# A planned attention-and-mixer kernel: a new order with two transfer lanes, V's parts and the output weights issued in pieces

## The chip, the cores and the metric

One core of a Trainium2 chip runs the kernel. The metric is the device time of an execution in microseconds; of several runs the median counts. Profiles come from one execution each, taken by the hardware profiler; its span is shorter than its time by what lies around the program.

## The reference

Four batches, 8 heads, 768 steps, head width 48. For each head a state of 48 x 48 decays by `w` at each step and takes in an outer product of `k` and `v`; the output reads the state with `r`, and the present step with the bonus `u`:

```
cur = u * k_t (outer) v_t
y_t = r_t @ (state + cur)
state = w_t * state + k_t (outer) v_t
```

The heads of `y` are laid side by side as `x` (4 x 768 x 384), and a token mixer follows: `wq = x @ w_q`, `wk = x @ w_k` (width 64), weights `wq @ wk.T / 8`, `mixed = weights @ x`, and `out = relu(mixed) @ w_out`. All inputs and the output are float32.

## The kernel before

The sequence is cut into 12 units of 256 steps (3 to a batch), each with two chunks of 128 steps. A unit loads 384 KB each of w, k, r and v (`wg`, `kg`, `rg`, `vg`; a partition holds two neighbouring steps of all heads). Then, per unit n:

- ACT takes the logarithm of w (`ln.n`, tile `lw`), PE sums it over time (`cw.n`), ACT makes two exponentials of the sums (`ep.n`, `en.n`).
- k, r and v are cast to bf16 (`k16.n`, `r16.n`, `v16.n`, mostly on POOL); PE turns k and r (`kT.n`, `rT.n`) and brings v into step order (`vp.n`, copied out as `VB.n`).
- DVE or POOL form the decayed factors: `ks`, `qT`, `RT`, `KT`. PE multiplies them (`A.n.c`), DVE masks the result (`AM.n.c`); `kb`, `kd`, `sn` and `SB` carry the state; `dps`, `dd` and `Vd` are the bonus term; `yi` (state) and `ya` (inside the chunk) are added to `Vd` as `X.n`.
- `X` is turned (`xt`, `XT`) and projected (`qk`, `QK` or `wqc`, `wkc`). After the third unit of a batch, `T` and `TS` (keys times x) follow, and for each unit of the batch `mx`, `rl` (relu, tile `MX`), `fp` (times `w_out`), `os` (copy out of PSUM) and the store `st`. A mixer unit `mx.m` uses the same numbers 0 to 11.

Unit 0 and unit 11 do some steps by chunk. Every wide matmul group has several ways, chosen by a letter: whole ("E") or as two halves of 64 columns ("e", "f").

All this is recorded as steps of a `Plan`. Each step names the engines that could do it with a cost in ns, the steps that it waits for, and the buffers that it reads and fills. Two tables hold the result of a search: `ALT`, a letter for the engine or way of each step that has a choice, and `RANK`, a place for each step. `Plan.order` sorts each engine's queue by rank, replays the queues with the costs, hands out PSUM banks, and so writes the program's order. Engines run their queues strictly in order; at run time only semaphores count, the costs do not.

All loads and nearly all stores are issued by SP, in one queue (`S`). A load may be issued once the cast of the unit four before has released its buffer (rings of four). In the plan a transfer is three steps: the issue on SP, the wire (`Q`) and the landing (`L`, 1950 ns). The old plan has a second wire lane (`R`) that is moved on by a fixed amount at each block of 128 PE instructions, and holds SP when the third-last transfer hasn't moved yet.

For units 2 to 11 V is loaded in three DMAs by partitions, 0 to 63, 64 to 126 and 127, one behind another. The weights `w_q`, `w_k` and `w_out` are three DMAs of one step (`wts`); POOL casts them (`wcast`). Thirty matmuls on a tile of zeros (`z`) are steps of the plan that keep PE busy early on.

Of the kernel before, what the change touches and what calls it, by code (L numbers as in the profile page):

```python
# [33 lines left out]
class Plan:  # L34
# [8 lines left out]
    ASIDE, BLOCKED = 1200, 1000  # L43
# [45 lines left out]
    def dma(self, key, issue, dur, fn, after=(), buf=None, reads=(), behind=None, high=None):  # L89

        i = self.add(key, {"S": issue}, fn, after, buf, lag=0, behind=behind)
        m = self.add(key + ("wire",), {"Q": (dur, dur if high is None else high, None)}, None, [i], lag=0)
        l = self.add(key + ("land",), {"L": self.LAND}, None, [m], lag=0, reads=reads)
        return i, l

    def order(self):
# [5 lines left out]
        wires = {}  # L102
# [6 lines left out]
        owners, moved, done, mode = [None] * 8, [], [], 0  # L109
# [14 lines left out]
        def start(s):  # L124
# [7 lines left out]
            if s["eng"] == "S" and len(moved) >= 3:  # L132
                t = max(t, moved[-3])
# [30 lines left out]
        while True:  # L164
# [5 lines left out]
            s = queues[e][place[e]]  # L170
# [24 lines left out]
            if lock:  # L195
                took += max(0, free["P"] - t)
            run(s, t, took)
            if lock:
                free["P"] = max(free["P"], t + took)
            if s["i"] in wires:  # L200
                m = wires[s["i"]]
                free["Q"] = max(free["Q"], s["end"]) + m["dur"]
                free["R"] = max(free["R"], s["end"]) + m["mode"]
                m["start"], m["end"] = s["end"], max(free["Q"], free["R"])
                done.append(m)
                moved.append(m["end"])
# [44 lines left out]
]  # L251
ALT = ("DDEDPEAEAPPEEEDEAeeEEeADPAEDPPeAEAPEEEAeEEEEDAPPEEEDPAeAEAPEEEAeEEEDAAEAEAEAEAEAEAPPEEED"
       "PPeAEDPEEEAeEEEEAAAPEEEAPAeDEAPEEEDEeEEEDAPPEEEAPPeAEAPEEEAEEEEDADEAEAEAEAEAeAPPEEEDPPEA"
       "EDPEEEAeeEEEDAPPEEEDPAEAEAPEEEAeeEEEDAPPEEEDPPeAeDPEEEAEEEEADAEAEAEAeDEAeDPPEEEDPPeAEAPE"
       "EEDeEEEEAAPPEEEDPPEAEDPEEEAEEEEeADPPEEEDPeAeDDPEEEAEEEEDDDeADDAeAEAeEDAeAeDEEDAeAeAEEDAE"
# [6 lines left out]
def kernel(  # L262
# [99 lines left out]
    def load(b, i, tl, ap, cuts=(0, C)):  # L362
        for p, z in zip(cuts, cuts[1:]):
            nc.sync.dma_start(  # L364
                out=view(tl, 0, [[D2, H], [1, D2]], p0=p, pn=z - p),
                in_=ap[b, :, ds(i * U + 2 * p, 2 * (z - p))].rearrange("h (p j) d -> p h (j d)", j=2))
# [114 lines left out]
    def weights():  # L481
        bq = Buf("none")

        def f(e):
            nc.sync.dma_start(out=view(wq_f, 0, [[DH, NK], [1, DH]]),
                              in_=moe_w_q.rearrange("(n p) h -> p n h", p=128))
            nc.sync.dma_start(out=view(wk_f, 0, [[DH, NK], [1, DH]]),
                              in_=moe_w_k.rearrange("(n p) h -> p n h", p=128))
            nc.sync.dma_start(out=view(wo_f, 0, [[DM, NK], [1, DM]]),
                              in_=moe_w_out.rearrange("(n p) d -> p n d", p=128))  # L490
        l = plan.dma(("wts",), 1800, 2700, f)[1]
# [5 lines left out]
        wts["qk"] = wts["o"] = add(("wcast",), {"P": 2650}, cast, [l])  # L497
# [7 lines left out]
    def unit(n, batch):  # L505
# [9 lines left out]
        for name, ap in (("wg", w), ("kg", k), ("rg", r)) + (() if whole else (("vg", v),)):  # L515
            g[name] = ring(name)
            cuts = (0, 64, 127, C) if name == "vg" and n in SPARE else (0, C)
            g[name + "L"] = plan.dma((name, n), 570 * (len(cuts) - 1) if "S" in begun else 1055,
                                     1220 if len(cuts) == 2 else 1730,
                                     lambda e, ap=ap, x=g[name].tile, cuts=cuts: load(b, i, x, ap, cuts),  # L520
                                     buf=g[name], behind=begun.get("S") if n == 0 else None,
                                     high=1220 if len(cuts) == 2 else 610)
# [162 lines left out]
        else:  # L685
# [4 lines left out]
                view(g["vg"].tile, 0, [[D2, H], [D, 2], [1, D]])), [g["vgL"]], v16, [g["vg"]])  # L690
# [244 lines left out]
        for ii in range(NU):  # L935
# [39 lines left out]
            for cs in halves:  # L975
# [8 lines left out]
                else:  # L984
                    plan.dma(("st", m, cs[0]), 400, 480 * len(cs), f_st, oss[cs], reads=[o])
# [70 lines left out]
```

## Time and profile before

| | |
|---|---|
| median of 3 runs | 106.12 us (105.59 to 106.23) |
| profiled execution | 106.6 us, span 104.8 us |
| busy share PE, PEld, DVE, ACT, POOL | 87, 63, 80, 76, 64% |
| share of the span in which the chain goes through PE, DMA, SP's queue | 38, 26, 9% |
| read and written in HBM | 19.66 and 4.72 MB |
| granted TensorE clock | 0.984 |

PE's busy time includes the `z` matmuls (39 of 128 x 512, 14.1 us). The chain is the work that ended last, followed back from the end: at each step to what released it. Times in the views are microseconds from the span's start, and "x3" counts instructions that a row merges. "Slices" are the 40 equal parts of the span on the page.

### The profile page before, as it was taken

Reading aid. Unit: us, or ns where it says so; the run is one execution under the profiler, and the core shown is the slowest. Engines: PE = TensorE matmul, PEld = TensorE weight load, DVE = VectorE, ACT = ScalarE, POOL = GpSimd, SP = SyncE. Lnnn points to the kernel's source line nnn. Section 1 sums busy time; section 2 is a strip of 40 time slices with the busy share of each in tenths; the row PEclk is TensorE's granted clock in tenths of the full one; section 3 lists DMA queues with packets and bytes.
Section 4 is the critical chain, followed back from the end, with each engine's and each line's share of the span. In section 5 each row is a group of like instructions: output and inputs, shape, how many; then the busy total and the mean of one; then the engine's idle time right before and its main releaser. Section 6 shows DMA issues by size and latency. Waiting matters only on the chain.

```text
span 104.8 us, 5072 instructions
## 1 busy us (share of the span) xinstructions
PE 91.6 (87%) x2201; PEld 65.7 (63%) x2201; DVE 84.3 (80%) x152; ACT 80.0 (76%) x117; POOL 66.9 (64%) x70
## 2 busy tenths in 40 slices
PE   6999998887699789999589689998999999999940
PEld 2264885485567558786375577865777778787510
DVE  5539999898699939999789699998999899857630
ACT  4359879989777298795996988999959898873830
POOL 4433695978998936988589779779995910400000
PEclk9999999999999957999999999999999999999999
DMA  1999997989999999889898999999989100029784
GB/s 33 317 323 325 325 318 183 282 228 244 264 315 267 235 298 248 215 199 280 226 228 199 248 304 307 222 317 301 304 283 326 43 0 6 6 111 367 274 287 172
DMA packets 53488, 24.71 MB, mean 236 GB/s; under 512 B 51162, under 2 KB 52314, under 8 KB 53466
## 3 DMA queue, kind: packets, MB, share of 16 engines
q1 hardware_dynamic: 53306, 24.19, 83.4%
q8 instruction: 17, 0.28, 1.1%
q10 hardware_dynamic: 160, 0.20, 0.5%
q14 instruction: 5, 0.04, 0.1%
HBM read 19.66 MB, written 4.72 MB: 233 GB/s over the span
## 4 chain that ended last, share of the span: by engine, by line
PE 38%; DMA 26%; SPq 9%; ACT 8%; POOL 6%; issue 5%; DVE 4%; POOLq 0%; ACTq 0%; DVEq 0%
PE PS L306 38%; DMA wg<-in_w_dram 13%; DMA vg<-in_v_dram 8%; SPq L364 8%; DMA kg<-in_k_dram 5%; ACT MX L466 3%; DVE AM L746 2%; POOL r L547 2%; POOL k L547 2%; POOL Vd L725 1%; ACT os L454 1%; ACT en L595 1%; SPq L977 1%; DVE VB L460 1%; ACT lw L536 1%
## 5 line engine op out<-in xcount | busy, mean ns | idle before, releaser
L746 DVE TENSOR_TENSOR AM<-PS,US 128x1024 bf16<-128x1024 f32 x24 | 29.0, 1220 | 2.8 <-PE PS L306 2.8
L725 POOL TENSOR_TENSOR Vd<-VB,dd 128x768 bf16<-128x768 bf16 (+1 forms) x13 | 17.6, 1353 | 8.3 <-DVE dd L460 6.1
L663 POOL TENSOR_TENSOR KT<-ks,en 128x1024 bf16<-128x1024 bf16 x10 | 21.3, 2129 | 0.8 <-ACT ep L589 0.7
L595 ACT ACTIVATE en<-PS,dn 128x1024 bf16<-128x1024 f32 (+1 forms) x14 | 13.9, 992 | 2.9 <-PE PS L306 2.4
L306 PE MATMUL PS<-Z 128*128 128x512 bf16 (+1 forms) x43 | 14.8, 432 | 1.1 <-DVE Z L380 1.0
L536 ACT ACTIVATE lw<-wg 128x768 bf16<-128x768 f32 x12 | 10.1, 842 | 6.3 <-DMA wg<-in_w_dram 6.2
L589 ACT ACTIVATE ep<-PS,up 128x1024 bf16<-128x1024 f32 (+1 forms) x14 | 13.9, 1011 | 1.0 <-PE PS L306 0.8
L306 PE MATMUL PS<-wo,MX 128*128 128x384 bf16 (+1 forms) x93 | 13.8, 327 | 0.3 <-ACT MX L466 0.3
L306 PEld LDWEIGHTS <-KT 48*128 48x128 bf16 x352 | 9.1, 95 | 6.9 <-issue 4.0
L547 POOL CAST k<-kg 128x768 bf16<-128x768 f32 x10 | 8.3, 825 | 6.0 <-DMA kg<-in_k_dram 4.7
L851 DVE TENSOR_TENSOR X<-PS,Vd 128x768 bf16<-128x768 f32 (+1 forms) x13 | 11.5, 892 | 0.7 <-PE PS L306 0.4
L306 PE MATMUL PS<-RT,KT 48*128 48x128 bf16 x192 | 9.9, 220 | 1.4 <-ACT QK L454 0.9
L466 ACT ACTIVATE MX<-PS 128x768 bf16<-128x768 f32 (+1 forms) x14 | 9.4, 700 | 1.9 <-PE PS L306 1.9
L687 POOL CAST v<-vg 128x768 bf16<-128x768 f32 x9 | 7.4, 827 | 4.3 <-DMA vg<-in_v_dram 4.1
L547 POOL CAST r<-rg 128x768 bf16<-128x768 f32 x10 | 8.3, 827 | 2.3 <-DMA rg<-in_r_dram 2.3
L650 DVE TENSOR_TENSOR RT<-PS,ep 128x1024 bf16<-128x1024 bf16 (+1 forms) x14 | 8.4, 607 | 1.6 <-PE PS L306 1.4
L454 ACT CAST VB<-PS 128x768 bf16<-128x768 f32 x11 | 8.9, 807 | 1.0 <-issue 0.6
L454 ACT COPY os<-PS 128x768 f32<-128x768 f32 (+1 forms) x10 | 7.0, 702 | 3.3 <-PE PS L306 2.1
L306 PEld LDWEIGHTS <-MX 128*128 128x128 bf16 (+1 forms) x93 | 7.1, 103 | 3.5 <-ACT MX L466 0.4
L306 PE MATMUL PS<-CM,lw 64*128 64x128 bf16 x192 | 8.2, 231 | 1.2 <-ACT lw L536 1.0
L641 DVE TENSOR_TENSOR qT<-PS,ks 128x1024 bf16<-128x1024 bf16 x12 | 8.2, 683 | 0.4 <-PE PS L306 0.3
L809 DVE TENSOR_TENSOR SB<-PS,ep 128x192 bf16<-128x192 f32 x20 | 7.0, 350 | 1.8 <-PE PS L306 1.7
(88 smaller groups left out, 184.9 us busy)
## 6 DMA issues: line engine op xcount, KB each, us to landing
wg<-in_w_dram SPq DMA_DIRECT2D x12, 384.0 KB
kg<-in_k_dram SPq DMA_DIRECT2D x12, 384.0 KB
rg<-in_r_dram SPq DMA_DIRECT2D x12, 384.0 KB
out_dram<-os SPq DMA_DIRECT2D x9, 384.0 KB
vg<-in_v_dram SPq DMA_DIRECT2D x10, 192.0 KB
vg<-in_v_dram SPq DMA_DIRECT2D x10, 189.0 KB
out_dram<-os SPq DMA_DIRECT2D x5, 192.0 KB
vg<-in_v_dram SPq DMA_DIRECT2D x2, 384.0 KB
```

Source lines behind the costliest of these rows:

```text
L306: return nc.tensor.matmul(o, l, rr, start=start, stop=stop, skip_group_check=True, is_transpose=trans)
L454: nc.scalar.copy(o, i)
L466: nc.scalar.activation(o, i, ACT.Relu)
L536: nc.scalar.activation(view(lw.tile, 0, [[64, H], [512, 2], [1, D]]), view(g["wg"].tile, 0, [[D2, H], [D, 2], [1, D]]), ACT.Ln, bias=0.0, ...
L547: op(view(o.tile, 0, [[64, H], [512, 2], [1, D]]), view(g[src].tile, 0, [[D2, H], [D, 2], [1, D]]))
L589: nc.scalar.activation(view(ep.tile, cs[0] * NP * EW + RS, [[EW, n4], [1 - RS, 2], [1, R]]), view(at(cw), cs[0] * 512, [[C, n4], [R, 2], [ ...
L595: nc.scalar.activation(en.tile[:, ds(cs[0] * 512, w_)], at(cw)[:, ds(cs[0] * 512, w_)], ACT.Exp, bias=dn, scale=-1.0)
L650: nc.vector.tensor_tensor(view(RT.tile, cs[0] * 512, [[512, len(cs)], [R, H], [1, R]]), view(at(kr, BF16), cs[0] * apart + second, [[apart ...
L663: x.tensor_tensor(KT.tile[:, w], ks.tile[:, w], en.tile[:, w], ALU.mult)
L725: (nc.vector if e == "D" else nc.gpsimd).tensor_tensor(Vd.tile[:, cols], VB.tile[:, cols], view(dd.tile, cs[0] * H, [[1, len(cs) * H], [0, ...
L746: AMs[c] = add(("AM", n, c), {"D": 1221}, lambda e, c=c, A=A: nc.vector.tensor_tensor(view(AM[c].tile, 0, [[C, 8], [1, C]]), view(at(A), 0 ...
L851: lambda e, c0=c0, nc_=nc_: nc.vector.tensor_tensor(view(X.tile, (2 * i + c0) * DM, [[D2, NP * nc_], [D, 2], [1, D]]), view(at(y), c0 * NP ...
```

## The change

The computation, the tiles and the rings stay. What changes:

- The plan's model of transfers: two lanes, each with a depth (`DEEP`); an issue on SP lasts until both lanes have room. A load takes 1220 ns on lane Q and 1500 on lane R, which stands for the slower engine; the fixed delay at each PE block goes.
- V's three parts are steps of their own, in the order 64 to 126 (`vl`), 127 (`vk`), 0 to 63 (`vg`), so that other transfers can stand between them. Only `vg` takes time on lane R.
- `w_out` is loaded in three DMAs, rows 0 to 62, 63 to 125, 126 to 127 of each of three blocks, as a step of its own (`wtso`) behind `w_q` and `w_k` (`wts`).
- `RANK` and `ALT` are new: the order of every engine and the choice of engine for many steps.

```
-    ASIDE, BLOCKED = 1200, 1000
+    DEEP = dict(Q=1850, R=2500)
...
-            if s["eng"] == "S" and len(moved) >= 3:
-                t = max(t, moved[-3])
...
-                    free["R"] = max(free["R"], cross + self.ASIDE) + self.BLOCKED
...
+            if s["i"] in wires:
+                m = wires[s["i"]]
+                x = t + took
+                full = [0]
+                for q, d in (("Q", m["dur"]), ("R", m["mode"])):
+                    if d:
+                        free[q] = max(free[q], x)
+                        full.append(free[q] + m["opts"]["Q"][5] * d // max(m["dur"], 1) - self.DEEP[q])
+                        free[q] += d
+                m["start"] = x
+                m["end"] = max([x] + [free[q] for q, d in (("Q", m["dur"]), ("R", m["mode"])) if d])
+                took = max(took, max(full) - t)
...
-            nc.sync.dma_start(out=view(wo_f, 0, [[DM, NK], [1, DM]]),
-                              in_=moe_w_out.rearrange("(n p) d -> p n d", p=128))
-        l = plan.dma(("wts",), 1800, 2700, f)[1]
+        def f_o(e):
+            for p, z in ((0, 63), (63, 126), (126, 128)):
+                nc.sync.dma_start(out=view(wo_f, 0, [[DM, NK], [1, DM]], p0=p, pn=z - p),
+                                  in_=moe_w_out.rearrange("(n p) d -> p n d", p=128)[ds(p, z - p)])
+        l = [plan.dma(("wts",), 1000, 700, f, deep=900, high=850)[1],
+             plan.dma(("wtso",), 1500, 3300, f_o, high=0, deep=800)[1]]
...
+            if name == "vg" and n in SPARE:
+                g["vl"] = [plan.dma(("vl", n), 500, 1065, lambda e, f=f: f(e, p0=64, p1=127),
+                                    buf=g[name], high=0)[1]]
+                g["vl"].append(plan.dma(("vk", n), 500, 20, lambda e, f=f: f(e, p0=127, p1=C),
+                                        buf=g[name], high=0)[1])
+                g["vgL"] = plan.dma((name, n), 500, 610, lambda e, f=f: f(e, p0=0, p1=64),
+                                    buf=g[name], high=750)
```

The order of SP's transfers that follows from the tables, by step (numbers are units; `v` in the old order is V in three parts from unit 2 on):

```
before: wg0 kg0 rg0 vg0 wg1 kg1 rg1 kg2 wg2 vg1 rg2 v2 wg3 wg4 kg3 v3 rg3 wts kg4 rg4 wg5 v4
  kg5 rg5 wg6 kg6 rg6 v5 v6 wg7 rg7 kg7 v7 wg8 v8 rg8 kg8 wg9 rg9 kg9 wg10 v9 wg11 kg10
  rg10 rg11 kg11 v10 st2 st1 v11 st0 st4 st6 st5 st3 st7 st8 st9.1 st9.0 st10.0 st11.1 st10.1
after:  wg0 kg0 rg0 vg0 wg1 kg1 vg1 rg1 kg2 wg2 vl2 rg2 vk2 vg2 rg3 wg3 wts kg3 wtso wg4 vl3
  vk3 vg3 kg4 rg4 vl4 wg5 vg4 vk4 kg5 rg5 wg6 kg6 rg6 vl5 vl6 vk6 vg5 vk5 vg6 wg7 rg7 kg7
  vl7 vk7 vg7 kg8 rg8 vl8 vk8 wg8 vg8 wg9 rg9 kg9 vl9 kg10 vl10 vk9 vk10 wg10 vl11 vg9
  vg10 rg10 rg11 wg11 kg11 vk11 vg11 st3 st0 st5 st4 st2 st6 st1 st7 st8 st9.0 st9.1 st10.0
  st11.1 st10.1
```

The last pieces of the other queues that the prediction speaks of (POOL, ACT, from the third-last unit's end on):

```
POOL before: v16.10 Vd.9 r16.11 v16.11 k16.11 Vd.10 Vd.11.1
POOL after:  v16.10 Vd.9 v16.11 r16.11 Vd.10 k16.11 Vd.11.0 Vd.11.1
ACT before:  ln.11 dd.9 os.3 os.4 kd.10 XT.8 VB.10 QK.7 en.11 ...
ACT after:   ln.11 os.3 XT.7 kd.10 os.4 QK.7 VB.10 ep.11 QK.8 ...
DVE after:   X.9 X.10 KT.11.0 ks.11 SB.10.1 RT.11.0 RT.11.1 KT.11.1 qT.11 kd.11 AM.11.0 SB.11.0 AM.11.1 X.11.0 X.11.1
```

KT of units 1, 3 and 7 stands on DVE and not on POOL; XT of units 1, 4, 5 and 7 on ACT and not on DVE (8 the other way); fp of ten units instead of four goes in halves.

More of the change, by code (lines that the diff above doesn't have):

```diff
@@ L87, in add, with dma @@
         return s
-    def dma(self, key, issue, dur, fn, after=(), buf=None, reads=(), behind=None, high=None):
+    def dma(self, key, issue, dur, fn, after=(), buf=None, reads=(), behind=None, high=None,
+            deep=None):
         i = self.add(key, {"S": issue}, fn, after, buf, lag=0, behind=behind)
         m = self.add(key + ("wire",), {"Q": (dur, dur if high is None else high, None)}, None, [i], lag=0)
+        m["opts"]["Q"][5] = dur if deep is None else deep
         l = self.add(key + ("land",), {"L": self.LAND}, None, [m], lag=0, reads=reads)
@@ L108, in order @@
         rings = {k: [] for k in self.rings}
-        owners, moved, done, mode = [None] * 8, [], [], 0
+        owners, done, mode = [None] * 8, [], 0
         count, edge, ready = 0, self.FIRST, 0
@@ L196, in order @@
                 took += max(0, free["P"] - t)
+            if s["i"] in wires:
[10 more added lines that the diff above has]
+                took = max(took, max(full) - t)
+                for q, d in (("Q", m["dur"]), ("R", m["mode"])):
+                    if d:
+                        free[q] = max(free[q], t + took)
+                        m["end"] = max(m["end"], t + took)
             run(s, t, took)
@@ L200, in order @@
             if s["i"] in wires:
[L201 to L204, printed above, removed]
                 done.append(m)
-                moved.append(m["end"])
                 x = wires[m["i"]]
@@ L216 @@
 RANK = [
[34 rows of a table removed]
-]
[L252 to L255, printed above, removed]
[36 rows of a table added]
+]
+ALT = ("DAeDPeAEDDDEeeAEAeeeEEADPAEDDPEAEAPEEEAeeEEEAAAPEEEDPPeAEDPEEEAeEEEDAAEAEAEAEAEAEAPAEEED"
+       "DPeAEAPEEEAEeEEEAAPPEEEAPAEDEAPEEEDeeEEEAAPPEEEAPPEAEDPEEEAEEEEAAAeAEAEAeAEAeAPPEEEDPPeA"
+       "EDPEEEAEEEEEDAPPEEEDDPEAEDPEEEAeeEEEAAPPEEEAPPEAEAPEEEAEEEEDAAEAEAeDeDeAeAPPEEEDPPeDEDPE"
+       "EEDeEEEeAAPPEEEDPPeAEDPEeEAEEEEeAAPPEEEDPeAEAPPEEEDEEEEAAAfDADAeAeAeeADeDEDeeADeDEDeeDAE"
        "EEEEEEEEEEEEEEEEEEEEEEEEEEEEE")
@@ L360, with load @@
     dn = const([C, 1], F32, "dn")
[L362 to L366, printed above, removed]
+    def load(b, i, tl, ap, p, z):
+        nc.sync.dma_start(
+            out=view(tl, 0, [[D2, H], [1, D2]], p0=p, pn=z - p),
+            in_=ap[b, :, ds(i * U + 2 * p, 2 * (z - p))].rearrange("h (p j) d -> p h (j d)", j=2))
     def load_whole(b, q, tl):
@@ L496, in cast @@
             nc.gpsimd.tensor_copy(wo_sb, wo_f)
-        wts["qk"] = wts["o"] = add(("wcast",), {"P": 2650}, cast, [l])
+        wts["qk"] = wts["o"] = add(("wcast",), {"P": 2650}, cast, l)
         ut = bank()
@@ L516, in unit, with f @@
             g[name] = ring(name)
[L517 to L522, printed above, removed]
+            def f(e, ap=ap, x=g[name].tile, p0=0, p1=C):
+                load(b, i, x, ap, p0, p1)
+            t, issue, rest = 1220 if n < 2 else 1500, 500 if "S" in begun else 1055, None
+            if name == "vg" and n in SPARE:
[5 more added lines that the diff above has]
+                                    buf=g[name], high=750)
+            else:
+                g[name + "L"] = plan.dma((name, n), issue, 1220, f, buf=g[name], high=t,
+                                         behind=begun.get("S") if n == 0 else None)
             if n == 0:
@@ L689, in unit @@
                 view(v16.tile, 0, [[D, H], [DM, 2], [1, D]]),
[L690 removed]
+                view(g["vg"].tile, 0, [[D2, H], [D, 2], [1, D]])), [g["vgL"]] + g.get("vl", []), v16,
+                [g["vg"]])
             def f_vp(e):
@@ L984, in unit @@
                 else:
-                    plan.dma(("st", m, cs[0]), 400, 480 * len(cs), f_st, oss[cs], reads=[o])
+                    plan.dma(("st", m, cs[0]), 400, 480 * len(cs), f_st, oss[cs], reads=[o],
+                             deep=80 * len(cs), high=560 * len(cs))
     batch = None
```

70 rows, old and new, of the table RANK are left out of this document.

## The prediction

> **What bounds the kernel now.** I read the page first (busy shares, slices, queues), then the chain that ended last, then the time lines of SP, POOL, ACT and DVE around the places that the chain names, and the order in which both programs' instructions stand on each engine.
>
> ```profile
> span 104.8 us, 5072 instructions
> PE 91.6 (87%) x2201; PEld 65.7 (63%) x2201; DVE 84.3 (80%) x152; ACT 80.0 (76%) x117; POOL 66.9 (64%) x70
> ...
> GB/s 33 317 323 325 325 318 183 282 228 244 264 315 267 235 298 248 215 199 280 226 228 199 248 304 307 222 317 301 304 283 326 43 0 6 6 111 367 274 287 172
> ...
> q8 instruction: 17, 0.28, 1.1%
> ```
>
> No engine is full; the transfers lead. One slice is 104.8/40 = 2.62 us; counted from 0, slices 1 to 5 run at about 325 GB/s, slices 6 to 30 mostly do not: their shortfalls against 325 add up to 1603 GB/s, and 1603/325 x 2.62 = 12.9 us of holes before the last input has landed. The 17 packets of the instruction queue took 1.1% of 16 engines' span, 0.011 x 16 x 104.8 = 18.4 us, over 1 us each; the views don't part the sixteen engines, so that one or two carry them is an assumption here.
>
> ```profile
> 27.62 8.40 DMA wg<-in_w_dram
> ...
> 44.80 4.94 DMA wg<-in_w_dram
> ...
> 55.70 5.12 DMA kg<-in_k_dram
> ...
> 76.68 4.35 DMA vg<-in_v_dram
> ...
> 81.18 0.06 POOL v L687
> ...
> 81.95 0.84 POOL k L547
> ...
> 82.83 3.39 PE PS L306 x94
> ```
>
> The chain (start, us, what) goes through loads again and again and leaves them for good at 76.68 + 4.35 = 81.03, when the last part of unit 11's V lands. POOL then casts V and K, and PE takes K. After 81.03 there are 23.8 us of pure computation and stores.
>
> ```profile
> 5.37 1.15 SPq L364 DMA_DIRECT2D kg<-in_k_dram  x1
> 6.56 1.15 SPq L364 DMA_DIRECT2D rg<-in_r_dram  x1
> ...
> 17.54 2.54 SPq L364 DMA_DIRECT2D kg<-in_k_dram  x1
> ...
> 25.51 0.49 SPq L489 DMA_DIRECT2D wof<-in_moe_w_out_dram  x1
> ...
> 73.88 1.45 SPq L977 DMA_DIRECT2D out_dram<-os  x2
> 75.38 1.99 SPq L364 DMA_DIRECT2D vg<-in_v_dram  x3
> 77.41 24.22 SPq L977 DMA_DIRECT2D out_dram<-os  x12
> ```
>
> SP's own time line (start, us): in the steady stretch a 384 KB load is issued every 6.56 - 5.37 = 1.2 us, the pace of the wire (393 KB at 325 GB/s is 1.21 us). An issue of 2.54 us is SP held by a full queue; nothing behind it can be issued, though other DMA engines may be idle. That is how holes arise. Two stores stand ahead of the last V.
>
> **The change part by part.**
>
> *Stores leave the load stream.* The new SP order has all 14 of its stores behind the last load; before, two of 384 KB stood ahead of it. Two times 1.21 us off the wire: the last V lands 2.4 us earlier (lower bound the 1.45 us of SP). The stores that move to the end are covered by a wire that is nearly empty (slices 31 to 34: 43, 0, 6, 6).
>
> *Output weights in three.*
>
> ```profile
> wof<-in_moe_w_out_dram SPq DMA_DIRECT2D x1, 576.0 KB
> ```
>
> 590 KB at 325 GB/s is 1.8 us. The trace has no such pieces alone. If the 63-row pieces are slow, the nearest rows are the slices in which V's three-part loads stand thickest, at 199 GB/s: 590/199 = 3.0 us, or +1.2. If they bypass an engine that also fetches instructions, that engine gains up to its 1.8 us. Two more issues at 0.49 are +1.0 us of SP, hidden while the queue is full. I take 0, with ends -1.8 and +1.2.
>
> The Trainium skill (DMA: Bandwidth & Descriptors, "Why a DMA increments its semaphore by 16 and not by 1") says that such a copy uses the largest number of engines up to 16 that divides the slowest dimension on both sides, so 63 rows run on nine; an estimate by it is 1.8 x 126/128 x 16/9 = 3.2 us on those nine and nothing on the other seven, beside the 3.0 us from the 199 GB/s slice. The same page's "Rules for kernel authors" calls a split of a transfer over partitions useless and wants one of 128 partitions; by that rule this part is the +1.2. The low rate of the slices with V in parts speaks for it, the slow instruction queue against it.
>
> *Parts of V issued apart, new load order.* The 63-row part now goes first, often with another load before the 64-row part (vl.4, wg.5, vg.4; vl.9, kg.10, vl.10). SP should be held less by one lagging engine. What this is worth can only be bounded: nothing of the 12.9 us of holes, or all that the computation could follow:
>
> ```profile
> 10.00:90.00 80.00, 72.19 (x1926) 54.10 (x1926) 71.50 (x110) 67.25 (x97) 61.45 (x53) 0.98 0.90 238
> ```
>
> DVE (the third figure) is idle 80 - 71.5 = 8.5 us between 10 and 90, so that is the ceiling. Against that, the q and k weights now precede unit 3's K, the output weights its V, and wg.11 comes late: a loss of a load or so, up to 1.5 us, is possible. I take 1.5 us gained, nearer the low end, since every load still moves the same bytes.
>
> *Work moved between engines.*
>
> ```profile
> L663 POOL TENSOR_TENSOR KT<-ks,en 128x1024 bf16<-128x1024 bf16 x10 | 21.3, 2129 | 0.8 <-ACT ep L589 0.7
> ...
> L454 ACT COPY XT<-PS 128x768 bf16<-128x768 bf16 x5 | 4.0, 794 | 0.2 <-PE PS L306 0.2
> ...
> L650 DVE TENSOR_TENSOR RT<-PS,ep 128x1024 bf16<-128x1024 bf16 x10 | 6.8, 684 | 1.6 <-PE PS L306 1.4 <-issue 0.3
> ...
> L460 DVE COPY XT<-PS 128x768 bf16<-128x768 bf16 x6 | 3.3, 551 | 0.1
> ```
>
> KT of units 1, 3 and 7 goes from POOL (3 x 2.13 = 6.4 us less) to DVE. DVE on two SBUF operands isn't in the trace; between 0.68 (RT) and POOL's 2.13 I take 0.7, as DVE's other 1024-column products do: +2.1. Four whole XT go to ACT and one comes back: 3 x 0.55 = 1.65 off DVE, 3 x 0.79 = 2.4 on ACT. The small casts and relus (0.2 to 1.0 us each) about cancel on DVE. So DVE gains under 1 us, ACT some 3, POOL loses over 6; with 8.5 and 12.8 us idle between 10 and 90, DVE and ACT hide this (if ACT's cover is gone, up to 3 us).
>
> *The order at the end.*
>
> ```profile
> 79.22 0.82 POOL L547 CAST r<-rg 128x768 bf16<-128x768 f32 x1
> 81.18 0.83 POOL L687 CAST v<-vg 128x768 bf16<-128x768 f32 x1 [1.13 <-DMA vg<-in_v_dram]
> 81.95 0.83 POOL L547 CAST k<-kg 128x768 bf16<-128x768 f32 x1
> 82.74 1.48 POOL L725 TENSOR_TENSOR Vd<-VB,dd 128x768 bf16<-128x768 bf16 x1
> ...
> 75.13 0.83 ACT L536 ACTIVATE lw<-wg 128x768 bf16<-128x768 f32 x1
> ...
> 78.81 0.82 ACT L456 ACTIVATE kd<-PS 128x768 bf16<-128x768 bf16 x1
> 79.52 0.81 ACT L454 COPY XT<-PS 128x768 bf16<-128x768 bf16 x1
> 80.19 0.83 ACT L454 CAST VB<-PS 128x768 bf16<-128x768 f32 x1
> ...
> 89.07 0.80 ACT L454 COPY os<-PS 128x768 f32<-128x768 f32 x1 [0.25 <-PE PS L306]
> ...
> 86.35 0.96 DVE L851 TENSOR_TENSOR X<-PS,Vd 128x768 bf16<-128x768 f32 x1 [0.15 <-PE PS L306]
> 87.22 0.35 DVE L809 TENSOR_TENSOR SB<-PS,ep 128x192 bf16<-128x192 f32 x1
> ...
> 90.01 0.17 DVE L460 COPY dd<-PS 128x16 f32<-128x16 f32 x1
> 90.21 0.56 DVE L725 TENSOR_TENSOR Vd<-VB,dd 128x384 bf16<-128x384 bf16 x1
> 91.03 1.02 DVE L851 TENSOR_TENSOR X<-PS,Vd 128x384 bf16<-128x384 f32 x2 [0.26 <-PE PS L306]
> ...
> 90.78 1.14 PE L306 MATMUL PS<-wo,MX 128*128 128x384 bf16 x6
> ```
>
> POOL waited only 1.13 us for the last V, so an earlier landing alone is worth 1.13. Its new order is v, r, Vd.10, k of unit 11: k now stands behind Vd.10, which needs VB.10 from ACT. ACT's new order puts os.3, XT.7, kd.10, os.4, QK.7 and VB.10 behind ln.11, which waits for wg.11; and wg.11 is now the load third from last, with only kg.11 and V's last half behind it (1.2 + 0.6 = 1.8 us).
>
> The sum: the last V lands at 81.03 - 2.4 - 1.5 = 77.1, wg.11 at 75.3. From ln.11 to the end of VB.10 ACT has 4.9 us of work (ln 0.83, four copies at about 0.70 from one start to the next, as 78.81 to 79.52, a smaller one below that, VB 0.83), so VB.10 ends at 80.2 (81.02 before). Vd.10 holds POOL until 81.65, k starts there instead of 81.95: 0.3 earlier. Behind K's transposes DVE now has X.10 and the last dd and Vd out of its way: from PE's start on K at 82.83 to the end of X.11 at 92.05 it took 9.2 us; without X.10 (0.87 from start to start) and the dd, Vd and waits between 90.01 and 91.03 (some 0.9), plus a kd (0.3), 7.7 are left: -1.5. On PE one fp of 1.14 us (fp.6) leaves the stretch ahead of T.11 and another (fp.7) enters the one behind it: they nearly cancel, I take +0.2. Together -0.3 - 1.5 + 0.2 = -1.6 on the span of 104.8: 103.2.
>
> The profiled execution took 106.6 us beside its span of 104.8, and the runs' median is 106.12 (105.59 to 106.23), so the forecast is 106.12 - 1.6 = 104.5. About 1% is what a measurement of this kernel tells from no change.
>
> **The rivals.**
>
> *wg.11 comes too late (slower).* Mechanism: ACT stands at ln.11 with VB.10 behind it, POOL at Vd.10 with K behind it, PE at kT.11. By the sum above, each us that the load stream loses delays kT.11 by one; the change breaks even when the last V lands at about 78.7. If the new order gains nothing, and loses 1.2 by the weights and 1.0 by loads that come late, the last V lands at 81.03 - 2.4 + 2.2 = 80.8, wg.11 at 79.0, VB.10 ends at 83.9, K starts at 85.4: +3.4 - 1.3 = +2.1, 108.2. For it: in the old stream five more loads, two stores and a V stood behind wg.11, now hardly two; against it: the stores are gone.
>
> *Nothing comes through (same).* The split and the new order buy nothing: the last V lands at 78.6 for the stores alone, wg.11 at 76.8, VB.10 ends at 81.7, K starts at 83.1: +1.2 - 1.3 = -0.1, 106.0. For it: the same bytes go through the same engines, and the 2.4 us fall into a POOL that waited 1.13. Against it: the holes that SP's long issues show.
>
> *The holes close (much faster).* If half of DVE's 8.5 idle us between 10 and 90 go, the end comes 4 us earlier: 102.1. For it: chain pieces of 8.40, 4.94 and 5.12 us in loads. Against: seven stores of 384 KB and six of 192 KB then stand on SP from st.5 on, and os.5 was done at 89.07 + 0.80; at the 367 GB/s of slice 36 their 3.9 MB take 10.7 us, so the span can hardly end before 101.
>
> **How the numbers follow.** Forecast 104.5 (0.36), slower rival 108.2 (0.29), same at about 106 (0.20), holes close 102.1 (0.15). The range 102.0 to 108.2 takes in the unknown bounds of the order (-1.5 to +4 us around none); the likeliest case's own range is 103.4 to 105.2. Faster by over 1%: 0.36 + 0.15 = 0.51; within: 0.20; slower: 0.29.
>
> **What would show it.** Right: in the new profile no store before the last V, V of unit 11 landed by 77.5, wg.11 before 75.5, POOL's k of unit 11 started before 82, fewer slices under 250 GB/s. Wrong: ln.11 with a wait of more than 2 us for wg, the last V after 78.7, ACT or PE waits of several us around the weights at 22 to 30 us, or a tail behind kT.11 as long as before.

## The result, and the profile after

The new kernel takes 112.45 us (median of 4 runs, 110.96 to 113.24), the old one beside it 106.18: the ratio is 1.056 [1.042, 1.071], slower. The forecast was 104.5, with 108.2 as the end of the range.

The profiled execution took 113.24 us, 0.8 above the median, with a span of 111.4. Its first loads, of the same size as before, already ran slower (counted from 0, slice 3 at 253 GB/s, before 325), so the sizes are taken from the comparisons of medians below and only the places from this profile. A ratio leaves out runs that lie over 1.5% above the fastest of their kernel, so it can differ from that of the medians shown. The page's lines on span, engines, granted clock and transfers, and the shares of the chain by engine:

```profile
span 111.4 us, 5210 instructions
PE 93.9 (84%) x2272; PEld 67.9 (61%) x2272; DVE 84.4 (76%) x151; ACT 82.6 (74%) x121; POOL 60.4 (54%) x67
PEclk9999999999996569999999997699999999999999
GB/s 42 320 296 253 306 232 209 281 277 203 134 210 290 188 250 243 296 181 226 303 175 288 234 249 218 218 185 246 305 273 152 150 6 0 201 286 234 173 363 169
SPq 37%; DMA 22%; PE 21%; POOL 7%; issue 6%; ACT 3%; DVE 0%; POOLq 0%; ACTq 0%
```

The engines have nearly as much to do as before (PE and ACT 2.3 and 2.6 us more, DVE the same), and POOL 6.5 us less, about as counted. What grew is the part of the chain in which SP stands in an issue: 37% against 9% before. The new hole is at slice 10 (28 us): 134 GB/s.

The chain of waits (start, us, what):

```profile
25.38 4.87 SPq L375
...
72.11 3.69 DMA wg<-in_w_dram
...
76.62 6.32 DMA wg<-in_w_dram
...
82.96 0.34 ACT lw L558
...
95.11 12.60 PE PS L318 x298
```

Before, the chain left the loads with the last V. Now it leaves them with unit 11's gate weights, which land at 76.62 + 6.32 = 82.94, and goes on through ACT's logarithm and then through PE. POOL's cast of unit 11's K, which stood in it before, is no longer in it. SP's time line shows the two issues around the output weights, and the 14 stores behind the last load:

```profile
22.24 1.80 SPq L503 DMA_DIRECT2D wof<-in_moe_w_out_dram  x3
...
24.61 6.35 SPq L375 DMA_DIRECT2D vg<-in_v_dram  x3
...
79.69 1.99 SPq L375 DMA_DIRECT2D vg<-in_v_dram  x2
84.52 24.13 SPq L1000 DMA_DIRECT2D out_dram<-os  x14
```

ACT's time line, unit 5's logarithm and the end, and then POOL's end, the same instructions as in the prediction's fence:

```profile
41.16 0.84 ACT L558 ACTIVATE lw<-wg 128x768 bf16<-128x768 f32 x1 [0.98 <-DMA wg<-in_w_dram]
...
82.96 0.85 ACT L558 ACTIVATE lw<-wg 128x768 bf16<-128x768 f32 x1 [0.46 <-DMA wg<-in_w_dram]
...
87.63 0.80 ACT L465 CAST VB<-PS 128x768 bf16<-128x768 f32 x1
```

```profile
86.50 0.82 POOL L709 CAST v<-vg 128x768 bf16<-128x768 f32 x1
87.27 0.83 POOL L569 CAST r<-rg 128x768 bf16<-128x768 f32 x1
88.51 1.48 POOL L748 TENSOR_TENSOR Vd<-VB,dd 128x768 bf16<-128x768 bf16 x1 [0.41 <-ACT VB L465]
89.93 0.82 POOL L569 CAST k<-kg 128x768 bf16<-128x768 f32 x1
```

From K's start to the end of the span it is 111.4 - 89.93 = 21.5 us (before 104.8 - 81.95 = 22.9): the tail did get shorter. K starts 8.0 us later than before.

### The profile page after: what moved, and what is told of

It is laid out like the page before. It is cut to its first block, busy times and chain, and to the rows that moved or that the text cites. A ratio compares the mean times of both kernels' runs of the same rounds, so it can differ in the third digit from the quotient of the medians.

```text
span 111.4 us, 5210 instructions
## 1 busy us (share of the span) xinstructions
PE 93.9 (84%) x2272; PEld 67.9 (61%) x2272; DVE 84.4 (76%) x151; ACT 82.6 (74%) x121; POOL 60.4 (54%) x67
## 4 chain that ended last, share of the span: by engine, by line
SPq 37%; DMA 22%; PE 21%; POOL 7%; issue 6%; ACT 3%; DVE 0%; POOLq 0%; ACTq 0%
SPq L375 34%; PE PS L318 21%; DMA wg<-in_w_dram 9%; DMA kg<-in_k_dram 5%; DMA rg<-in_r_dram 4%; DMA vg<-in_v_dram 4%; POOL KT L685 2%; SPq L503 2%; POOL r L569 1%; SPq L496 1%; POOL Vd L748 1%; POOL k L569 1%; ACT lw L558 1%; POOL v L709 1%; ACT os L465 1%
## 5 line engine op out<-in xcount | busy, mean ns | idle before, releaser
L318 PE MATMUL PS<-Z 128*128 128x512 bf16 (+2 forms) x45 | 15.5, 431 | 1.1 <-DVE Z L391 1.0
L685 POOL TENSOR_TENSOR KT<-ks,en 128x1024 bf16<-128x1024 bf16 x7 | 14.9, 2130 | 2.6 <-ACT ks L465 1.6
L318 PE MATMUL PS<-wo,MX 128*64 128x384 bf16 (+1 forms) x114 | 13.7, 328 | 0.0
L709 POOL CAST v<-vg 128x768 bf16<-128x768 f32 x11 | 9.1, 826 | 8.2 <-DMA vg<-in_v_dram 7.5
L318 PE MATMUL PS<-CM,lw 64*128 64x128 bf16 (+1 forms) x208 | 7.9, 231 | 5.4 <-ACT lw L558 2.9
L318 PEld LDWEIGHTS <-KT 48*128 48x128 bf16 (+1 forms) x376 | 9.5, 98 | 3.9 <-issue 1.6
L318 PE MATMUL PS<-RT,KT 48*128 48x128 bf16 (+1 forms) x208 | 9.8, 224 | 0.6 <-POOL KT L685 0.5
L318 PEld LDWEIGHTS <-lw 64*128 64x128 bf16 (+1 forms) x208 | 6.2, 105 | 6.7 <-ACT lw L558 5.0
L318 PEld LDWEIGHTS <-MX 128*64 128x64 bf16 (+1 forms) x114 | 7.1, 106 | 3.3 <-issue 0.2
L477 ACT ACTIVATE MX<-PS 128x768 bf16<-128x768 f32 (+1 forms) x10 | 7.4, 750 | 1.9 <-PE PS L318 1.9
```

Of the source, the lines that this page charges most:

```text
L318: return nc.tensor.matmul(o, l, rr, start=start, stop=stop, skip_group_check=True, is_transpose=trans)
L685: x.tensor_tensor(KT.tile[:, w], ks.tile[:, w], en.tile[:, w], ALU.mult)
L709: v16s = add(("v16", n), {"P": 826, "A": 810}, lambda e: (nc.scalar.copy if e == "A" else nc.gpsimd.tensor_copy)(view(v16.tile, 0, [[D, H] ...
```

## The experiments

Each kernel is the one before or after with one part exchanged. "Loads" means the order on SP; the engines' order (PE, ACT, DVE, POOL, with the choice of engine) goes apart from it. Every ratio is to the kernel before, run beside it on the same chip. None leaves work out.

### 1 to 4: pieces, loads, engines

**1. After, output weights whole.**

```
-            for p, z in ((0, 63), (63, 126), (126, 128)):
+            for p, z in ((0, 128),):
```

> The changed kernel with w_out loaded in one DMA of 128 rows at the place of the three; all orders else kept. Weights theory (the two 63-row pieces hold the load stream for some 3 us between 24 and 30 us, and all that follows is late by it): 108 to 110 us, SP is not held for 4.9 us behind them, wg of unit 4 lands near 29 instead of 31.7. Order theory (the new order of engines and loads costs the time wherever the weights stand): 111.5 to 113, as the changed kernel.

110.51 us (109.48 to 111.05), ratio 1.040 [1.031, 1.050]. The kernel after stood at 1.056 [1.042, 1.071]. So the pieces look like a part of the loss and not the whole of it; but the two intervals overlap, and run 2 is the clearer measure.

**2. Before, output weights in pieces.** The same edit the other way round, in the kernel before.

> The kernel before with nothing changed but w_out in the three DMAs of the change. Weights theory: 108 to 109.5 us, K of unit 4 lands 2 to 3 us later than at 31.25. Order theory: 105.5 to 106.8, since the DMA engines have room there.

110.77 us (110.03 to 111.58), ratio 1.045 [1.036, 1.054]. This one edit, counted at nothing, costs 4.6 us, more than either theory had. POOL's time line, first of the kernel before, then of this one:

```profile
30.87 1.15 POOL L496 CAST wo<-wof 128x1152 bf16<-128x1152 f32 x1
32.49 0.83 POOL L547 CAST r<-rg 128x768 bf16<-128x768 f32 x1 [0.47 <-DMA rg<-in_r_dram]
```

```profile
32.89 1.15 POOL L497 CAST wo<-wof 128x1152 bf16<-128x1152 f32 x1 [1.40 <-DMA wof<-in_moe_w_out_dram]
37.24 0.83 POOL L548 CAST r<-rg 128x768 bf16<-128x768 f32 x1 [3.20 <-DMA rg<-in_r_dram]
```

The weights' cast is 2.0 us late, but the R behind them 4.75. The landing records of the trace (one for each part of a transfer, sixteen for a load of 128 rows) divide this in two. The whole stream is shifted: K of the same unit is 2.55 us late, and fifteen of R's sixteen parts 2.3 (34.64 against 32.37). R's last part comes only at 37.19, 2.55 behind the fifteen. Such a late part is not the pieces' own: in before, the last part of unit 5's gate weights landed 2.1 us behind the others (36.02 against 33.93). SP's time line, of before and of this kernel, shows why the loss spreads:

```profile
27.62 2.34 SPq L364 DMA_DIRECT2D wg<-in_w_dram  x1
30.06 2.71 SPq L364 DMA_DIRECT2D vg<-in_v_dram  x3
```

```profile
26.04 1.24 SPq L490 DMA_DIRECT2D wof<-in_moe_w_out_dram  x3
...
28.49 3.89 SPq L364 DMA_DIRECT2D wg<-in_w_dram  x1
32.47 4.91 SPq L364 DMA_DIRECT2D vg<-in_v_dram  x3
```

The issues of the pieces are short; the two loads behind K and R hold SP for 3.89 and 4.91 us instead of 2.34 and 2.71. The view of the transfers from 24 to 34 us, of the kernel before and of this one:

```profile
DMA packets 6403, 2.77 MB, mean 277 GB/s; under 512 B 6017, under 2 KB 6401, under 8 KB 6401
```

```profile
GB/s 223 197 237 246 264 287 289 208 146 65 60 241 172 90 48 107 135 197 233 227 203 234 253 301 233 221 181 183 198 174 157 171 206 298 321 297 237 224 284 293
DMA packets 4583, 2.08 MB, mean 208 GB/s; under 512 B 4197, under 2 KB 4581, under 8 KB 4581
```

In the last of these rows V's second and third part are issued only by 35.77 and 37.38 (R's late part landed at 37.19), so the loads behind them go out 4.6 us later than before; a delay of mostly 3 to 5 us stays to the end. In the same 10 us 0.69 MB less went over, 2.5 us at the old rate, and the quarter-microsecond slices fall to 48 GB/s around the pieces.

**3. After, with the loads of before** (V's parts in the old order too, output weights whole).

```
-RANK: SP's entries in the new order; V as 64 to 126, 127, 0 to 63
+RANK: SP's entries in the order of before; V as 0 to 63, 64 to 126, 127
```

> The changed kernel's order on PE, ACT, DVE and POOL, with SP's whole sequence of the kernel before (same loads, same parts of V in the old order, w_out whole, stores at their old places). Load theory (the new sequence of transfers is what costs, not the engines' order): within 1.5 us of before, 105 to 107.5. Order theory: 110 or more, since engines wait in their new order for data that comes in the old one.

Ratio 1.016 [1.010, 1.022], from 107.6 and 107.8 us (the other two of the four runs took 111.0 and 113.4). The engines' order by itself is no gain but a loss of about 1.6%.

**4. Before, with the loads of after** (pieces included): SP's entries and V's parts exchanged the other way.

> The other half of the cross: the engines' order of the kernel before with the changed kernel's whole sequence on SP, pieces of w_out and V included. Load theory: 110 to 113, as slow as the changed kernel. Order theory: 106 to 108.

114.18 us (113.34 to 114.46), ratio 1.076 [1.069, 1.082]: worse than after. The new loads cost the old engines' order 7.6%; given these loads, the new engines' order looks the better one by about 2%, though the intervals overlap a little.

### 5 to 8: which part of the load order

**5. Before, V's 63-row part first.**

```
-        for p, z in zip(cuts, cuts[1:]):
+        for p, z in ((64, 127), (127, C), (0, 64)) if len(cuts) > 2 else ((0, C),):
```

> The kernel before, with one edit: V's three parts of each unit are issued as rows 64 to 126, row 127, rows 0 to 63 in one go, the 63-row part first as after the change. Prediction's own step (SP is held less when the 63-row part goes first): the issues of V on SP shrink and the time is 105.0 to 106.0. Rival (the order of the parts is no matter, the losses of the new load order come from which loads stand where): 105.9 to 106.6, within 0.5% of before. If the part order itself is what makes the late loads slow: 107.5 or more, with the last V landing after 82.5 instead of 81.0.

106.08 us (105.11 to 107.5), ratio 0.989 [0.982, 0.997]. The part order is a gain of about 1%. That it comes by SP being held less, as the prediction's step had it, is not shown: SP's issues of V's parts add up to 23.5 us in this profile and to 26.3 in before, but those of the other loads to 45.1 against 43.3, and this one execution (span 105.2) is no faster than the one of before.

**6. Before, the two stores behind the last V.**

```
-... v10 st2 st1 v11 st0 ...
+... v10 v11 st2 st1 st0 ...
```

> The kernel before, with the two stores that stood ahead of unit 11's V moved behind it; every other engine as before. Prediction's step: the last V lands 2.4 us earlier (78.6 instead of 81.03) and the time falls by the 1.1 us for which POOL waited for it: 105.0. Rival (the two stores only filled time in which the wire or SP's queue was held by something else): the last V lands within 0.7 us of 81.0 and the time stays at 106.1 within 0.5%.

106.45 us (104.74 to 107.81), ratio 0.987 [0.978, 0.997]. The gain in time is near the 1.1 us expected, but not by the way expected. Lines of POOL's end in this kernel:

```profile
77.79 0.82 POOL L687 CAST v<-vg 128x768 bf16<-128x768 f32 x1 [1.06 <-DMA vg<-in_v_dram]
...
80.88 0.83 POOL L687 CAST v<-vg 128x768 bf16<-128x768 f32 x1
81.65 0.83 POOL L547 CAST k<-kg 128x768 bf16<-128x768 f32 x1
```

By the trace's landing records the last V is there at 80.68, 0.35 earlier and not 2.4. But this is one late part again: of the nine parts of V's 63 rows eight are there at 79.10, before at 80.72, so most of the V did come 1.6 us earlier. POOL could not use it: it now waits 1.06 us for unit 10's V instead, whose last part is late too, and takes the last V without a wait. K starts 0.3 earlier and the span is 0.4 shorter in this pair of profiles. The busy times and rates from 75 to 80 us, of before and of this kernel (the last column is GB/s):

```profile
75.00:80.00 5.00, 4.96 (x93) 3.54 (x90) 4.85 (x8) 3.72 (x7) 5.00 (x4) 1.00 0.93 308
```

```profile
75.00:80.00 5.00, 4.96 (x99) 3.58 (x97) 4.82 (x9) 3.72 (x7) 3.94 (x4) 1.00 0.84 265
```

With the stores behind the loads, less went over in these 5 us, (308 - 265) x 5 us = 0.21 MB: a part of the room that they left stayed empty.

**7 and 8. Half of the load order each.** Engines of after, output weights whole; the loads through unit 7 new and the rest old (7), or the other way round (8).

```
 7: ... vg7   -kg8 rg8 vl8 vk8 wg8 vg8 wg9 rg9 kg9 vl9 kg10 ...   +wg8 v8 rg8 kg8 wg9 rg9 kg9 wg10 v9 wg11 ...
 8: -wg1 kg1 vg1 rg1 kg2 wg2 vl2 ... wts kg3 wtso ...   +wg1 kg1 rg1 kg2 wg2 vg1 rg2 v2 ... wts wtso kg4 ...   v7
```

> The kernel after, output weights in one transfer (as in the first experiment, 110.5), and the loads of units 8 to 11 and the stores in the order of before; through unit 7 the loads keep the new order. Theory 'late' (the new order of the last units' loads, with the gate weights behind K, R and half of V, makes ACT wait and is what costs 2.8 us between the first and third experiment): 107.5 to 108.5. Theory 'early' (the new order through unit 7, q and k weights ahead of unit 3's K, costs it): 110 to 111. If both halves share it: 109.

> The mirror of the run before it: engines of after, output weights in one transfer, loads through unit 7 in the order of before, those of units 8 to 11 and the stores in the new order. Theory 'late': 110 to 111, with the last unit's gate weights landing after 77 and the last V after 80. Theory 'early': 107.5 to 108.5. If both halves share it: 109.

7: 109.21 us (108.08 to 110.34), ratio 1.019 [1.010, 1.028]. 8: 108.16 us (106.68 to 109.33), ratio 1.004 [0.993, 1.015], which rests on two of four runs. Neither came near the 1.040 of run 1, so neither theory held; but this was another chip than that of runs 1 to 4.

### 9 to 12: both gains, halves, gates

**9. Before, edits 5 and 6 together.**

> The kernel before with both small edits of the second batch: the two stores behind unit 11's V, and V's 63-row part issued first, row 127 and the 64-row part behind it. If the two gains of about 1% (0.989 and 0.987 against before, each with an interval of 0.8 to 0.9%) are real and apart: ratio 0.975 to 0.980, about 104. If they are one and the same (both only end the wait of POOL for the last V): 0.985 to 0.990. If they were the spread of the runs of before on that chip: 1.00.

105.31 us (104.03 to 107.68, 12 runs), before 106.36 (17 runs), ratio 0.992 [0.987, 0.997]. The gains do not add up: 0.989 x 0.987 would be 0.976, and the two together are no better than either alone on its own chip. That both only end POOL's wait for the last V fits the profile, in which POOL takes it at 80.56, 1.2 us after its landing at 79.37 and without a wait; it is not proved by it.

**10. Before, output weights in two halves.**

```
+            for p, z in ((0, 64), (64, 128)):
```

> The kernel before with the output weights in two transfers of 64 rows (in the second experiment: 63, 63 and 2 rows, 110.8 us, +4.7). Theory 'rows' (63-row pieces run on nine or ten engines, so the pieces keep those busy while the others stand idle and SP is held behind them): 106.1 within 1%, packets of 1536 B as short as before (mean 73 ns), the pieces landing within 2.2 us of each other. Theory 'count' (each further transfer on the one queue costs): half the added transfers, half the cost, about 108.4.

107.78 us (107.43 to 109.07), ratio 1.019 [1.011, 1.026]. The transfers from 24 to 34 us:

```profile
DMA packets 5527, 2.44 MB, mean 244 GB/s; under 512 B 5141, under 2 KB 5525, under 8 KB 5525
```

0.33 MB less than whole, about half of the three pieces' 0.69, and about 40% of their cost in time. The packets of the output weights took a mean of 108 ns (73 whole, 96 in three pieces), so they are not as short as theory "rows" wanted. Each 64-row half lands in sixteen parts by the trace, as a whole transfer does, a 63-row piece in nine (a tenth record comes right behind its issue, 0.2 us after it ends, and is no data). What the nine do to the stream stands in the profile of after, in quarter-microsecond slices from 24 to 34 us:

```profile
DMA  9996666597999999997878886666666849999999
GB/s 303 318 286 212 203 167 166 166 208 174 214 217 227 237 257 187 146 117 98 104 117 101 89 158 180 180 181 181 183 180 194 140 92 264 313 281 257 270 309 309
```

From 30.0 to 31.5 the DMA engines are busy to six tenths and move 180 to 183 GB/s, and 9/16 of 325 is 183. By this estimate nine work and the others have nothing, since SP stood in one issue from 25.38 to 30.26. So a second transfer costs by itself (run 10), and the third with the odd row counts costs more than that again; that the rows are a part of it is seen in these slices, but how much is the count and how much the rows, two points do not part.

The Trainium skill (DMA: Bandwidth & Descriptors, "Rules for kernel authors") advises against two transfers of partition halves, since both go over the same engines, and wants one of 128 partitions. This run agrees, and here the split is not neutral but costs 1.9%. By the same page of the Trainium skill ("Why a DMA increments its semaphore by 16 and not by 1") 63 rows run on nine engines; the estimate by it was 3.2 us in place of 1.8. The number of parts agrees, and the direction too; by the landing records of run 2 it took longer, 4.6 us from the landing ahead to that of the second piece (28.2 to 32.8), where the whole transfer took 1.6 (28.5 to 30.1).

**11. After, output weights whole, gate weights ahead.** Units 8, 10 and 11 alone.

```
-kg8 rg8 vl8 vk8 wg8 vg8 wg9 rg9 kg9 vl9 kg10 vl10 vk9 vk10 wg10 vl11 ... rg10 rg11 wg11 kg11
+wg8 kg8 rg8 vl8 vk8 vg8 wg9 rg9 kg9 wg10 vl9 kg10 vl10 vk9 wg11 vk10 vl11 ... rg10 rg11 kg11
```

> The kernel after with the output weights in one transfer (first experiment) and one more edit: the gate weights of units 8, 10 and 11 are issued ahead, in the places that they had between the other loads before (wg.8 first of its unit, wg.10 behind unit 9's K, wg.11 behind unit 10's K and V's 63-row part); all other loads and all engines as in that experiment. Theory 'gates' (rival of the prediction: ACT stands at ln with VB behind it, POOL at Vd): the lost 2.5% come back, ratio 1.015 to 1.02 as in the run with the load order of before, ln.11 at 75 to 76 instead of 78.5. Theory 'stream' (the whole stream of units 8 to 11 is late, and to have gates first only makes K, R and V later): 1.035 to 1.045, with POOL's waits for R and K longer by what ACT's wait for the gates falls.

111.86 us (109.52 to 115.12), ratio 1.039 [1.025, 1.053]: no gain against run 12 (the intervals overlap), and above the 1.015 to 1.02 of theory "gates", which falls. That late gate weights are only a sign of a late stream fits, but half of its sign is missing: in this profile ACT's waits for the gates are 3.8 us against 6.1 in run 12 and POOL's for R 4.4 against 2.8, but those for K 3.1 against 4.0. Its further sizes are not read, since the granted clock sank to 0.67 from 79 to 82 us.

**12. Run 1 again, beside it.**

> The first experiment's kernel again (after with the output weights in one transfer), beside the run above on one chip, as its measure and as that of the two runs in which half of the loads has the order of before (1.019 and 1.004 on another chip). If the ratio to before is the same on every chip: 1.03 to 1.05. If it comes out at 1.02 or less, the first batch overstated the load order's part by what is missing.

109.37 us (107.9 to 110.45), ratio 1.024 [1.014, 1.035], lower than run 1 on another chip. ACT's logarithms of units 5 and 11 and POOL's V and K of unit 11, in two views:

```profile
36.55 0.84 ACT L558 ACTIVATE lw<-wg 128x768 bf16<-128x768 f32 x1 [0.15 <-DMA wg<-in_w_dram]
...
78.14 0.84 ACT L558 ACTIVATE lw<-wg 128x768 bf16<-128x768 f32 x1 [0.33 <-DMA wg<-in_w_dram]
```

```profile
81.81 0.83 POOL L709 CAST v<-vg 128x768 bf16<-128x768 f32 x1
...
83.68 1.48 POOL L748 TENSOR_TENSOR Vd<-VB,dd 128x768 bf16<-128x768 bf16 x1 [0.27 <-ACT VB L465]
85.11 0.82 POOL L569 CAST k<-kg 128x768 bf16<-128x768 f32 x1
```

ACT's line of unit 5 in the kernel before:

```profile
36.10 0.84 ACT L536 ACTIVATE lw<-wg 128x768 bf16<-128x768 f32 x1 [2.01 <-DMA wg<-in_w_dram]
```

The logarithm of unit 5 starts at 36.55, nearly as before; in the profile of after it starts at 41.16. Of these 4.6 us 1.1 stood already ahead of the pieces (the k weights landed at 24.64 in after, at 23.55 here), so the pieces put some 3.5 us in by unit 5; with them whole, 2.6 us come in later, between unit 5 and unit 11 (78.14 against 75.13). The chain of this run shows where:

```profile
67.22 4.21 DMA wg<-in_w_dram
71.52 0.85 ACT lw L558
...
76.18 9.20 PE PS L318 x277
...
86.95 15.99 PE PS L318 x361
```

It leaves the loads with unit 10's gate weights, not unit 11's, and from 76.18 PE works almost without a break. The rows from 60 us on, of before and of this run (PE's busy time is the first figure behind the length):

```profile
60.00:76.00 16.00, 15.23 (x420) 11.47 (x420) 14.95 (x24) 14.65 (x20) 13.64 (x12) 1.00 1.10 292
```

```profile
60.00:76.00 16.00, 11.54 (x338) 8.82 (x332) 12.27 (x18) 13.77 (x20) 10.45 (x9) 1.00 1.02 243
```

PE works 3.7 us less between 60 and 76, and then as much as before (13.65 of the 14 us to 90, before 13.67). So the time is lost ahead of the last loads. These are not late at the end: the last V landed at 79.94, earlier than the 81.03 of before.

### 13 to 16: the four load orders on one chip

Kernels 1, 3, 7 and 8 again, side by side, on the chip of runs 1 to 4.

> Engines of after, output weights in one transfer, load order new through unit 7 and new behind it; beside the three other corners on one chip. If the order costs: 1.5 to 2.5% above the corner old-old. If only the chips differed: within 0.7% of it.

> The corner with the whole load order of before (third experiment, 1.016 there). It measures what the order on the engines costs by itself: 1.010 to 1.022 if that run was typical, 1.00 if it was not.

> The corner with the new order through unit 7 and the old one behind it (1.019 on another chip). If the cost lies early: as corner new-new. If it lies late: as corner old-old.

> The corner with the old order through unit 7 and the new one behind it (1.004 on another chip, from two runs). If the cost lies late: as corner new-new. If it lies early: as corner old-old. If the two halves only cost together: both mixed corners as old-old, new-new alone above.

| loads through unit 7 / behind | us, median (range) of 6 runs | ratio |
|---|---|---|
| new / new | 109.74 (109.18 to 110.44) | 1.043 [1.035, 1.051] |
| old / old | 107.69 (106.71 to 109.82) | 1.020 [1.011, 1.029] |
| new / old | 108.57 (108.17 to 111.69) | 1.032 [1.024, 1.040] |
| old / new | 108.31 (105.65 to 111.55) | none: too spread |

On one chip the whole load order costs about 2% (1.043 against 1.020). Of this the early half bears about half, 1.2% (1.032 against 1.020), with intervals that overlap. The late half by itself could not be sized: its six runs lie anywhere from 105.65 to 111.55, and run 8 gave 1.004 for the same kernel. So whether the late half costs only behind the new early one is open. New / new and old / old repeat runs 1 and 3 on this chip (1.040 and 1.016); why the same kernel stood at 1.024 on run 12's chip stays open. POOL's end in the old / old run:

```profile
80.19 0.82 POOL L709 CAST v<-vg 128x768 bf16<-128x768 f32 x1 [0.87 <-PE PS L318]
80.96 0.83 POOL L569 CAST r<-rg 128x768 bf16<-128x768 f32 x1
81.75 1.48 POOL L748 TENSOR_TENSOR Vd<-VB,dd 128x768 bf16<-128x768 bf16 x1
83.17 0.82 POOL L569 CAST k<-kg 128x768 bf16<-128x768 f32 x1
```

The last V is cast 1.0 us earlier than before (POOL waits for PE there, not for the V), but K starts 1.2 later: R and Vd.10 now stand between them (2.98 us from V to K, before 0.77). The tail behind K is 104.6 - 83.17 = 21.4. In this one profile the two cancel against before's (104.6 and 104.8); the median does not (+2.0%). About 0.4 us of that lies outside the span (2.1 us in this run against 1.7 in those of before); where the rest lies is not shown.

## Why the prediction was wrong

The sum had a simple frame: unit 11's gate weights land, 6.35 us later K starts (ln to VB 4.9, Vd 1.45), and 21.55 us after that the span ends (22.85 - 1.5 + 0.2). In size the frame held, in both kernels of the table:

| | predicted | after | run 12, weights whole |
|---|---|---|---|
| gate weights of unit 11 land | 75.3 | 82.94 | 78.1 |
| from ln.11 to K's start | 6.35 | 6.97 | 6.97 |
| K's start to the end of the span | 21.55 | 21.5 | 21.5 |
| span | 103.2 | 111.4 | 106.6 |

Its path did not. K never keeps PE waiting for long in these two profiles (0.16 us ahead of K's transposes, and that for DVE), and in run 12 the chain goes neither through unit 11's gate weights nor through K: PE has lost its time before 76 us and is the engine that ends last. So the agreement of the two stretches is in part luck. By the ratios of runs 3 and 1 and of after the loss is made up of some 1.6% for the engines' order, 2.4% for the loads' order with the stores, and 1.6% for the pieces.

- **The order at the end: right in size.** From K's start the tail got 1.35 us shorter (22.85 to 21.5); -1.3 was said. It counts where K is on the path, as in run 14, where PE waits for K and the tail is 21.4. That X.10, dd and Vd out of DVE's way are the reason was not tested apart.
- **Output weights in three, taken as 0: the step that failed.** It measured +4.6 us in the kernel before and, in the new one, 1.9 (run 1) to 3.1 (run 12) between medians. The upper end of +1.2 was the price of the pieces' own bytes at 199 GB/s; in run 2 the weights are cast 2.0 us late, K lands 2.55 late and R 4.75. I had priced a transfer alone, not the queue behind it: SP held, the next loads issued late, and no slack in the stream to win it back. The relief that I set against it, an engine that also fetches instructions, did not show; R's last part landed 2.55 us behind its other fifteen by the trace's records, and which engine carried it the records don't say.
- **The new load order, taken as 1.5 gained: wrong sign.** It costs about 2% (13 against 14), though the stores, counted as a gain of their own, are in this. What was right in it is small: the 63-row part first is worth about 1% (5), in the old order of loads. I took the gain from SP's long issues, but the new order does not shorten them: SP's issues of loads add up to 69.6 us in before and to 69.7 in run 13. In run 12 it is the late gate weights of unit 10, issued behind K, two V parts and two single rows in the new order, at which the chain leaves the loads; but to issue them ahead gained nothing (11).
- **The stores, taken as -2.4 on the last V: mis-sized.** It is 0.35 by the last landing record (6) and 1.6 by those of all parts but the late one; the time gained 1.3% [0.3, 2.2], which the profile pair shows only in part. The step left out that the slowest of a transfer's parts decides, and that POOL would then wait for the V before.
- **Work moved between engines, taken as hidden: mostly wrong.** The engines' order with the old loads costs 1.6 to 2.0% (3, 14). I had priced the end of the order and POOL's relief, but in run 14 R and Vd.10 ahead of K on POOL take back 2.2 us (2.98 against 0.77) of what the tail gives; where the rest goes is open. KT on DVE took 0.68 us each, as the 0.7 had it; a DVE product of two SBUF operands was in the old trace after all (Vd at 90.21).
- **The rivals.** "wg.11 comes too late" named the right side, and in after the chain does go through wg.11; but from there it goes into PE and not through Vd.10 and K, and in run 12 it leaves the loads one unit earlier. Its price, 2.1, was too small since it left the pieces at 1.2, and its sign (a wait of over 2 us at ln.11) was not there: ln.11 waited 0.46, as ACT and PE were late themselves by then. Run 11 also speaks against its reason: with the gates ahead nothing was gained, and R was later. "Nothing comes through" and "The holes close" are out, since the time rose.

The signs for wrong that did appear: the last V at 84.73 by the landing records (over 78.7), and waits around the weights (28 to 34 us, below). The signs of a long wait at ln.11 and of an unchanged tail did not.

## What to carry to other kernels

A transfer that is cut into pieces is priced by the loads behind it on the queue, not by its own bytes: here 590 KB in three pieces made the following K 2.55 us late and R 4.75. Before calling bytes moved out of a stream a gain, look at the last part of the load behind them and at what its user would wait for next: here 2.4 us were counted, most parts came 1.6 earlier, and 0.3 reached the cast of K. A frame of "landing, then so many us to the end" can be right to 0.6 us and the forecast still be 8 us off, so ask the chain whether its path is taken at all; and the term with no row in the old profile deserves the widest bounds.

## What the runs showed of the hardware that I had not expected

One transfer of 128 rows, two of 64 and three of 63, 63 and 2 for the same 590 KB gave 106.1, 107.8 and 110.8 us (the second on another chip, ratio 1.019): a cost that the issues (1.24 us for three) do not show.

Behind the hole in the loads the granted clock went down. The stretches of after (PE's busy time is the first figure behind the length; the granted clock the third-last):

```profile
31.00:34.00 3.00, 1.44 (x43) 1.11 (x43) 1.58 (x3) 1.57 (x2) 0.92 (x1) 1.00 0.92 233
34.00:37.00 3.00, 1.91 (x21) 1.02 (x17) 0.76 (x2) 2.27 (x4) 1.81 (x3) 0.52 1.13 268
37.00:40.00 3.00, 3.00 (x90) 2.91 (x92) 2.58 (x3) 1.64 (x2) 2.11 (x2) 0.50 1.17 194
```

PE is busy for 1.44 of 3 us while the loads are late, and then works 6 us at 0.52 and 0.50. In run 12, with the weights whole, the clock stayed at 1.00 through these stretches. That the hole is the cause is not shown: before has such a stretch too, shorter (0.51 from 37 to 40), and run 10, with PE busy for 1.84 of 3 us from 31 to 34, has none right behind it. What the dip itself costs was not measured apart either; the four runs of after had spans of 109.1 us at a mean clock of 0.978 and of 110.6 to 111.4 at 0.953 to 0.958.
